# All attention first, then one feed-forward run over all batches, with the attention output through DRAM

## The chip, the cores and the metric

The kernel runs on one core of a Trainium2 chip. The core has five engines with an instruction queue each, which they work through in order: TensorE (PE, matrix multiplication; its weight loads are shown as PEld), VectorE (DVE), ScalarE (ACT), GpSimd (POOL) and SyncE (SP), which here only issues DMA transfers. The metric is the device time of one execution in microseconds (us); less is better.

## The reference

The computation has two parts. The first is attention in which a query sees only the keys of its own hash bucket; the second is a feed-forward layer with a short convolution as a gate. There are 4 batches, 8 heads, 768 positions, head size 64, a model width of 512 and an inner width of 1024.

```python
q_bucket = sum over 6 bits of ((q @ proj) > 0) * 2**bit     # k_bucket likewise
mask = q_bucket[:, :, :, None] == k_bucket[:, :, None, :]
scores = where(mask, q @ k.T / 8, -1e9)
attn = exp(scores - max(scores))
attn = attn / (sum(attn) + 1e-9)
x = (attn @ v) with the heads side by side                  # (4, 768, 512)
h = maximum(x @ w_in, 0)                                    # (4, 768, 1024)
conv = conv_w[0] * h[s-1] + conv_w[1] * h[s] + conv_w[2] * h[s+1]
out = (h * sigmoid(conv)) @ w_out
```

The weights `w_in`, `w_out` and `conv_w` come as 64-bit floats, which the kernel decodes on the chip from their integer halves.

## The kernel before

**Work units.** Two heads of a batch form a pair; there are 16 pairs. Each pair has 12 units: a unit is 128 queries of one head against all 768 keys. Units run in groups of four (two heads, two blocks of 128 queries), so a pair has three groups and the kernel 48 groups. The main loop has one iteration per unit, and in each iteration the engines work on different units: `products` (line 286, four matmuls `s`) and `maximum` (lines 299 to 303) of unit i, `normalise` (lines 313 and 314) of unit i-1, and `transposes` (line 329, six transposes `t`) and `to_sbuf` (line 336, ScalarE copies them out) of unit i-3. `exponential` (line 306) is on ScalarE. Once in a group, in the iteration after its last transposes, `values` multiplies the group's transposed probabilities with v: 24 matmul records `v` of line 355 in a row, the burst. All of this is issued in the order of the loop, and each engine takes its instructions in this order.

**PSUM.** The products `s`, the transposes `t` and the hash of the next pair take turns in three PSUM slots of two banks each (`ring(ps, 3, ..., "S", ...)`). So the transposes of an iteration take the slot that the maximum of the iteration before has read, or an older one: the transposes of the third iteration of a group wait for the maximum of its second.

**Two kinds of normalisation.** The first six pairs (`LATE = NP + DEFER`) do not normalise the probabilities. They collect the sums (`reciprocals`), spread the reciprocals by two transposes (line 350), and multiply the values by them (`factors`, `out`: lines 360 to 366). The other ten pairs normalise each unit on GpSimd (line 314, in place, 128 x 768) and copy the values out in a high and a low part (lines 369 and 372). Both forms leave the attention output in SBUF, as a high part `xh` and a low part `xl`.

**Preparation of the next pair.** During a pair, `prepare` works on the next: `split` rounds the queries and keys on GpSimd (line 204, `hi`), subtracts (line 209, `R`, in place: the remainder) and lets SP copy the parts into their operand tiles by DMA (lines 207 and 211); `hash` computes the bucket bits (lines 219 to 228). The pieces come at iterations 1, 3, 4, 5 and 7 of the 12. The keys and queries of the pair after next are loaded at iteration 7 into the only tile `R` (line 191), after the DMAs that still read it.

**Decoding.** `split_weights` is a generator that decodes 16 blocks of weights. A block takes four vector steps on VectorE (lines 95, 97, 102 and 104), a size and a rounding on ScalarE (lines 87 and 136), a clamp on GpSimd (line 90), and a subtraction and an addition on GpSimd (`ends`, lines 139 and 140), which are issued halfway through the next block. `background(RATE)` takes 3.75 steps in every burst iteration from iteration 7; the rest falls in the first feed-forward. `fetch` loads the raw blocks from ScalarE's queue.

**Feed-forward.** `ffn(b, ...)` runs after two pairs of the next batch have been done, so four times, between attention pairs. It has 16 steps, one for half of the positions and one of eight blocks of 128 inner columns. A step has `hidden` (line 393, 12 matmuls `h`, then ScalarE and VectorE for the gate, lines 398 to 411, then GpSimd, line 412) and, three steps later (`FLAG`), `output` (line 423, 9 matmuls `o` that add up in PSUM). At the start ScalarE loads the table of the sigmoid, at the end that of the exponential (line 435).

The loop's central lines:

```python
        if u:
            u.maximum(prev)
        ...
        if prev and prev.pair.late:
            prev.normalise()
        ...
        next(prep[0], None)
        for _ in range(1 + NCK if ending else AVS[(i - LAG) % 4]):
            ...                       # the burst: values
        if burst and i >= W0:
            background(RATE)
```

Of the kernel before, what the change touches and what calls it, by code (L numbers as in the profile page):

```python
# [17 lines left out]
P = 128  # L18
# [3 lines left out]
QB = 256  # L22
# [9 lines left out]
DEFER = 2  # L32
FLAG = 3
LATE = NP + DEFER
AVS = (1 + NCK, 0, 0, 0)
PREP = 1
PREP_N = 6
W0 = 7
RATE = 3.75
# [4 lines left out]
def lsh_attention_conv_ffn(ctx, tc, qk, v, hw, w_in, conv_w, w_out, consts, ident_in, out):  # L44
# [113 lines left out]
    fetched, due, taps = [], [0], []  # L158
# [10 lines left out]
    def background(n):  # L169

        due[0] += n
        while due[0] >= 1:
            due[0] -= 1
            next(weights_todo, None)


    class Pair:
        def __init__(self, b, p):
            self.b, self.p, self.nm = b, p, f"{b}_{p}"
            self.late = b * NP + p >= LATE  # L180
            self.rec = None
# [92 lines left out]
    class Unit:  # L274
# [14 lines left out]
        def maximum(self, prev):  # L289

            self.st = ring(wp, 8, [P, 4], F32, "st", f"st{self.nm}")
            pr = self.pair
            if self.tq == 0 and self.h == 0 and not pr.late:
                pr.sums = ring(wp, 3, [P, QB // P, 2], F32, "sums", f"sums{self.nm}")
            self.sums = None if pr.late else pr.sums
            self.sum = self.st[:, 2:3] if pr.late else pr.sums[:, self.tq, self.h:self.h + 1]
# [4 lines left out]
            if prev and prev.pair.late:  # L301
                prev.total()
            nc.vector.tensor_scalar(self.st[:, 1:2], self.st[:, 0:1], -SCALE, None, ALU.mult)  # L303

        def exponential(self):
            nc.scalar.activation(self.e, self.e, AF.Exp, bias=self.st[:, 1:2], scale=SCALE,  # L306
                                 accum_out=self.sum)

        def total(self):
            nc.vector.tensor_scalar(self.sum, self.sum, 1e-9, None, ALU.add)  # L310

        def normalise(self):
            nc.vector.reciprocal(self.st[:, 3:4], self.sum)
            nc.gpsimd.tensor_scalar(self.e, self.e, self.st[:, 3:4], 0.0, ALU.mult, ALU.add)  # L314

        def reciprocals(self):

            pr = self.pair
            sums = self.sums
            nc.vector.tensor_scalar(sums, sums, 1e-9, None, ALU.add)  # L320
            nc.vector.reciprocal(sums, sums)
            pr.rec = ring(wp, 1, [P, QB // P, 2, D], F32, "rec", f"rec{self.nm}")
            nc.gpsimd.tensor_scalar(pr.rec, sums.unsqueeze(3).to_broadcast([P, QB // P, 2, D]), 1.0, 0.0,
                                    ALU.mult, ALU.add)
# [14 lines left out]
    def values(pr, qb, ats, rec):  # L339

        if qb == 0:
            pr.x = [ring(wp, NP + DEFER, [P, S], F32R, f"x{k}", f"x{k}{pr.nm}")
                    for k in "hl"]
        vt, (xh, xl) = pr.v, pr.x
        av = ring(ps, 2, [P, 512], F32, "M", f"v{pr.nm}_{qb}")

        def spread():

            for t in range(QB // P):
                nc.tensor.transpose(av[:, QB + t * P:QB + (t + 1) * P],  # L350
                                    rec[:, t].rearrange("p h d -> p (h d)"), ident)

        def chunk(c):
            for h in range(2):
                nc.tensor.matmul(av[h * D:(h + 1) * D, :QB], vt[:, c, h, :],  # L355
                                 ats[h][:, c // 3, c % 3, :],
                                 start=(c == 0), stop=(c == NCK - 1), tile_position=(0, h * D))

        def factors():
            nc.scalar.copy(rs, av[:, QB:2 * QB])  # L360

        def out():
            x = ring(wp, 1, [P, QB], F32, "x32", f"x{pr.nm}_{qb}")
            nc.vector.tensor_tensor(x, av[:, :QB], rs, ALU.mult)
            nc.gpsimd.tensor_scalar(xh[:, cols], x, 1.0, 0.0, ALU.mult, ALU.add)
            nc.gpsimd.tensor_tensor(xl[:, cols], x, xh[:, cols].bitcast(F32), ALU.subtract)

        def out_high():
            nc.scalar.copy(xh[:, cols], av[:, :QB])

        def out_low():
            nc.vector.tensor_tensor(xl[:, cols], av[:, :QB], xh[:, cols].bitcast(F32), ALU.subtract)

        cols = slice(qb * QB, (qb + 1) * QB)
        chunks = [lambda c=c: chunk(c) for c in range(NCK)]
        if pr.late:
            return chunks, (out_high, out_low)
        rs = ring(wp, 1, [P, QB], F32, "rs", f"rs{pr.nm}_{qb}")
        return [spread, *chunks], (factors, out)


    g2, prep = [None], [iter(())]

    def hidden(b, half, f, xs):
# [4 lines left out]
        for c in range(NCC):  # L389
            xh, xl = xs[c]  # L390
# [23 lines left out]
    def output(b, half, f, g, acc):  # L414
        if f == 0:
            acc[half] = [ring(ps, 3, [P, 2, 512], F32, "S", f"o{b}_{half}_{k}")
                         for k in range(2)]
        for m in range(HS // P):
            op = acc[half][m // 2][:, m % 2, :]
            gh, gl = (g[:, k, m * P:(m + 1) * P] for k in range(2))  # L420
            wh, wl = (weights[f"o{f}"][:, k, :] for k in range(2))
            for n, (l, r) in enumerate(((gh, wh), (gh, wl), (gl, wh))):
                nc.tensor.matmul(op, l, r, start=(f == 0 and n == 0),  # L423
                                 stop=(f == NFC - 1 and n == 2))
        if f == NFC - 1:
            for m in range(HS // P):
                osb = ring(wp, 5, [P, WC], I32, "wl", f"osb{b}_{half}_{m}").bitcast(F32)
                copy = nc.vector.tensor_copy if m == 2 else nc.scalar.copy
                copy(osb, acc[half][m // 2][:, m % 2, :])
                r0 = half * HS + m * P  # L430
# [168 lines left out]
```

## Time and profile before

| | |
|---|---|
| median of 3 runs | 754.43 us (751.63 to 755.96) |
| span of the profiled execution | 749.0 us; its own device time is not listed apart from the three |
| TensorE | busy 714.4 us (95%), 4588 matmuls |
| VectorE, ScalarE, GpSimd | busy 499.2, 509.2 and 373.6 us |
| mean granted TensorE clock | 0.984 |
| DMA | 72.18 MB, mean 96 GB/s |

The span is from the first to the last instruction of the profile; the device time holds what lies around it as well. Lines of the profile name an engine, an operation, the tile written and the tile read, and numbers after `x` are counts. A `<-` in brackets after "idle before" names what ended an engine's wait. Matmuls are pipelined, so their single durations overlap; starts are the safer measure. "PE v L355 x24" is one burst.

### The profile page before, as it was taken

The page shows a single profiled execution, that of the slowest core. Times are in us where ns is not written, and L with a number is a line of the kernel's source. Part 1 is how long each engine was busy: PE and PEld are TensorE (multiplying, and loading weights), DVE is VectorE, ACT ScalarE, POOL GpSimd, SP SyncE. Part 2 cuts the span into 40 slices and gives each one's busy share as a digit, 9 for nine tenths or more (in the row PEclk, how much of TensorE's full clock was granted, in tenths as well). Part 3 has the DMA queues.
Part 4 walks back from the last instruction along what each step waited for, and adds up shares of the span by engine and source line. Part 5 has one row for each costly group of instructions (what it writes and reads, how often), then busy time and mean ns, then how long its engine had stood idle before and what let it go on. Part 6 is the DMA issues. An engine that isn't in the chain of part 4 may idle for free.

```text
span 749.0 us, 13385 instructions
## 1 busy us (share of the span) xinstructions
PE 714.4 (95%) x4588; PEld 587.5 (78%) x4588; DVE 499.2 (67%) x1195; ACT 509.2 (68%) x954; POOL 373.6 (50%) x372
## 2 busy tenths in 40 slices
PE   5989999988899999999999999999999999999997
PEld 3767777776679987777788988777788897778986
DVE  7588999977667656666657655665666665564663
ACT  5867887886655548778774557787785547785554
POOL 4366777756566324755735423656645323341221
PEclk8999999998999999999999999999999999999999
DMA  3876576553412102365441302255461211000011
GB/s 141 198 204 155 141 206 181 168 162 85 114 43 72 64 37 70 82 181 136 121 121 31 104 1 105 68 150 132 119 163 33 70 43 63 2 1 1 0 43 43
DMA packets 30357, 72.18 MB, mean 96 GB/s; under 512 B 5937, under 2 KB 7505, under 8 KB 30289
## 3 DMA queue, kind: packets, MB, share of 16 engines
q1 hardware_dynamic: 27696, 62.88, 30.9%
q10 hardware_dynamic: 2592, 8.44, 3.6%
q8 instruction: 37, 0.61, 0.3%
q14 instruction: 32, 0.25, 0.1%
HBM read 27.40 MB, written 6.29 MB: 45 GB/s over the span
## 4 chain that ended last, share of the span: by engine, by line
PE 69%; DVE 4%; POOL 4%; DMA 3%; ACT 1%; issue 1%; SPq 0%; POOLq 0%; DVEq 0%
PE o L423 18%; PE h L393 17%; PE s L286 11%; PE t L329 11%; PE v L355 11%; DVE e L299 2%; DMA k<-R 1%; DMA R<-in_qk 1%; PE hash L219 1%; POOL wuo L139 1%; POOL e L314 1%; POOL wo L140 1%; ACT e L306 1%; DVE wuo L97 1%; POOL R L209 1%
## 5 line engine op out<-in xcount | busy, mean ns | idle before, releaser
L299 DVE TENSOR_SCALAR_CACHE_REDUCE e<-s 128x768 f32<-128x768 f32 x192 | 183.3, 955 | 80.9 <-PE s L286 72.1
L306 ACT ACTIVATE e<-e,st 128x768 f32<-128x768 f32 x192 | 181.2, 944 | 23.1 <-DVE st L303 12.8
L336 ACT COPY at<-t 128x768 f32<-128x768 f32 x192 | 152.3, 794 | 47.3 <-PE t L329 47.1
L329 PE MATMUL t<-ident,e 128*128 128x128 f32 x1152 | 164.5, 280 | 19.9 <-DVE e L299 17.9
L314 POOL TENSOR_SCALAR e<-e,st 128x768 f32<-128x768 f32 x120 | 109.3, 911 | 117.3 <-ACT at L336 59.9
L329 PEld LDWEIGHTS t<-ident,e 128*128 128x128 f32 x1152 | 133.4, 144 | 42.6 <-DVE e L299 22.4
L402 DVE SCALAR_TENSOR_TENSOR ht<-ht,cw 128x384 f32<-128x384 f32 (+1 forms) x128 | 117.8, 921 | 70.0 <-ACT ht L400 66.8
L412 POOL TENSOR_TENSOR g<-ht,g 128x384 fp32r<-128x384 f32 x64 | 72.0, 1125 | 163.9 <-ACT g L411 129.7
L423 PE MATMUL o<-wo,g 128*128 128x512 f32 x576 | 143.3, 395 | 0.7 <-POOL g L412 0.7
L393 PE MATMUL h<-xh,wi 128*128 128x386 f32 x512 | 142.0, 340 | 0.0
L355 PE MATMUL v<-at,v 128*64 128x256 f32 x1152 | 134.9, 383 | 0.0
L423 PEld LDWEIGHTS o<-wo,g 128*128 128x128 f32 x576 | 107.0, 188 | 23.5 <-ACT ht L400 1.2
L286 PE MATMUL s<-K,Q 128*128 128x384 f32 x384 | 118.7, 391 | 1.0 <-POOL K L253 0.9
L355 PEld LDWEIGHTS v<-at,v 128*64 128x64 f32 x1152 | 78.7, 137 | 45.5 <-issue 10.9
L286 PE MATMUL s<-k,q 96*128 96x384 f32 x384 | 102.2, 348 | 2.2 <-DVE e L299 2.2
L405 ACT ACTIVATE ht<-ht 128x384 f32<-128x384 f32 x64 | 33.6, 525 | 96.4 <-DVE ht L402 96.4
L393 PEld LDWEIGHTS h<-xh,wi 128*128 128x128 f32 x512 | 94.0, 188 | 3.7 <-ACT ht L400 1.2
L393 PE MATMUL h<-xl,wi 128*128 128x386 f32 x256 | 86.8, 339 | 0.0
L286 PEld LDWEIGHTS s<-K,Q 128*128 128x128 f32 x384 | 60.1, 196 | 22.2 <-issue 17.4
L286 PEld LDWEIGHTS s<-k,q 96*128 96x128 f32 x384 | 72.9, 197 | 3.0 <-ACT q L266 3.0
L406 DVE TENSOR_TENSOR ht<-ht 128x384 f32<-128x384 f32 x64 | 41.5, 649 | 31.5 <-ACT ht L405 31.3
L209 POOL TENSOR_TENSOR R<-R,hi 128x768 fp32r<-128x768 f32 x30 | 60.4, 2014 | 0.9 <-PE hash L219 0.8
(75 smaller groups left out, 622.2 us busy)
## 6 DMA issues: line engine op xcount, KB each, us to landing
R<-in_qk SPq DMA_DIRECT2D x15, 768.0 KB
K<-hi SPq DMA_DIRECT2D x60, 192.0 KB
v<-in_v SPq DMA_DIRECT2D x16, 384.0 KB
out<-osb SPq DMA_DIRECT2D x24, 256.0 KB
Q<-hi SPq DMA_DIRECT2D x30, 192.0 KB
q<-hi SPq DMA_DIRECT2D x30, 192.0 KB
Q<-R SPq DMA_DIRECT2D x30, 192.0 KB
k<-R SPq DMA_DIRECT2D x30, 192.0 KB
```

The source lines that it names most:

```text
L209: nc.gpsimd.tensor_tensor(lo, R, hi.bitcast(F32), ALU.subtract)
L286: nc.tensor.matmul(self.sp[:, half, :HS], A[:, h, qs], C[:, h, half * HS:(half + 1) * HS], start=(kk == 0), stop=(kk == 1))
L299: nc.vector.tensor_scalar(self.e.rearrange("p (a b) -> p a b", a=2), self.sp[:, :, :HS], MASKED, None, ALU.max, ALU.max, accum_out=self.st ...
L306: nc.scalar.activation(self.e, self.e, AF.Exp, bias=self.st[:, 1:2], scale=SCALE, accum_out=self.sum)
L314: nc.gpsimd.tensor_scalar(self.e, self.e, self.st[:, 3:4], 0.0, ALU.mult, ALU.add)
L329: nc.tensor.transpose(self.tp[:, c // 3, c % 3 * P:(c % 3 + 1) * P], self.e[:, c * P:(c + 1) * P], ident)
L336: nc.scalar.copy(pr.at[self.h][:, :, :, self.tq * P:(self.tq + 1) * P], self.tp[:, :, :3 * P].rearrange("p j (c q) -> p j c q", c=3))
L355: nc.tensor.matmul(av[h * D:(h + 1) * D, :QB], vt[:, c, h, :], ats[h][:, c // 3, c % 3, :], start=(c == 0), stop=(c == NCK - 1), tile_posi ...
L393: nc.tensor.matmul(hp[:, :HW], w, x[:, c0:c0 + HW], start=(n == 0), stop=(n == 3 * NCC - 1))
L402: nc.vector.scalar_tensor_tensor(t[:, a:z], ht[:, o + k - 1 + a:o + k - 1 + z], cw[:, f, k:k + 1], t[:, a:z], ALU.mult, ALU.add)
L412: nc.gpsimd.tensor_tensor(g[:, 1, :], t, g[:, 0, :].bitcast(F32), ALU.subtract)
L423: nc.tensor.matmul(op, l, r, start=(f == 0 and n == 0), stop=(f == NFC - 1 and n == 2))
```

## The change

- All 16 pairs of attention run one after the other. All of them normalise each unit on GpSimd; the sums, the spreading and the factors of the first six pairs are gone.
- The output of a burst is copied once by VectorE (128 x 256), in the following iteration, and stored by SP to DRAM (`xd`).
- `feed_forward` is one run of 64 steps over all batches, started when the last products are issued, so that its first three steps stand among the last iterations of attention. It holds six output accumulators in the three PSUM slots, used half by half in turn.
- The attention output of a batch is loaded from DRAM by `load_x` and split into high and low parts by `split_x` on GpSimd: for the first batch during pairs 8 and 9, for the others during the feed-forward of the batch before.
- A step of the decoding is taken in every second iteration from iteration 14; a raw block is fetched in every sixth iteration.
- The tables are no longer switched back and forth between attention and feed-forward: the sigmoid's is loaded once.

```diff
-LATE = NP + DEFER
-AVS = (1 + NCK, 0, 0, 0)
-W0 = 7
-RATE = 3.75
+DECODE = 14
+FETCH = 6
+X0 = 8
...
     def exponential(self):
         nc.scalar.activation(self.e, self.e, AF.Exp, bias=self.st[:, 1:2], scale=SCALE,
-                             accum_out=self.sum)
+                             accum_out=self.st[:, 2:3])
...
-    def values(pr, qb, ats, rec):
+    def values(pr, qb, ats):
...
         def out():
-            x = ring(wp, 1, [P, QB], F32, "x32", f"x{pr.nm}_{qb}")
-            nc.vector.tensor_tensor(x, av[:, :QB], rs, ALU.mult)
-            nc.gpsimd.tensor_scalar(xh[:, cols], x, 1.0, 0.0, ALU.mult, ALU.add)
-            nc.gpsimd.tensor_tensor(xl[:, cols], x, xh[:, cols].bitcast(F32), ALU.subtract)
-
-        def out_high():
-            nc.scalar.copy(xh[:, cols], av[:, :QB])
-
-        def out_low():
-            nc.vector.tensor_tensor(xl[:, cols], av[:, :QB], xh[:, cols].bitcast(F32), ALU.subtract)
+            x = ring(wp, 2, [P, QB], F32, "x32", f"x{pr.nm}_{qb}")
+            nc.vector.tensor_copy(x, av[:, :QB])
+            nc.sync.dma_start(xd[pr.b][pr.p][:, qb * QB:(qb + 1) * QB], x)
...
+    def load_x(b):
+        xs = []
+        for c in range(NCC):
+            if b % 2 == 0:
+                x = ring(wp, NCC, [P, 2, S], F32R, "x", f"x{b}_{c}")
+            else:
+                x = ring(wp, 2, [P, 2, S], F32R, ("Q1", "K1")[c % 2], f"x{b}_{c}")
+            nc.sync.dma_start(x[:, 1].bitcast(F32), xd[b][c])
+            xs.append(x)
+        return xs
+
+    def split_x(xs):
+        for x in xs:
+            raw = x[:, 1].bitcast(F32)
+            nc.gpsimd.tensor_scalar(x[:, 0], raw, 1.0, 0.0, ALU.mult, ALU.add)
+            yield
+            nc.gpsimd.tensor_tensor(x[:, 1], raw, x[:, 0].bitcast(F32), ALU.subtract)
+            yield
...
+    def feed_forward(x0):
+        gs, run, xs, splits = [], [], x0, iter(())
+        load_table(AF.Sigmoid)
+        todo = [(b, half, f) for b in range(B) for half in range(2) for f in range(NFC)]
+        per = 2 * NFC
+        for i in range(len(todo) + FLAG):
+            if i % per == 0 and i < len(todo):
+                if i:
+                    xs = nxt
+                if i // per + 1 < B:
+                    nxt = load_x(i // per + 1)
+                    splits = split_x(nxt)
...
+            if i % per >= 4:
+                next(splits, None)
+            yield
...
-    for i in range(n + LAG):
+    for i in range(n + LAG + 1):
...
-        if burst and i >= W0:
-            background(RATE)
...
+        if i % FETCH == FETCH - 1:
+            fetch(1)
+        if i >= DECODE and i % 2 == 0:
+            next(weights_todo, None)
+        if pi == X0 and k == 0:
+            x0 = load_x(0)
+            splits = split_x(x0)
+        if x0 and k % 3 == 2:
+            next(splits, None)
+        if i == n:
+            tail = feed_forward(x0)
+        if tail:
+            next(tail)
```

More of the change, by code (lines that the diff above doesn't have):

```diff
@@ L300, in maximum @@
                                     MASKED, None, ALU.max, ALU.max, accum_out=self.st[:, 0:1])
-            if prev and prev.pair.late:
+            if prev:
                 prev.total()
@@ L384, in hidden @@
+            nc.vector.tensor_copy(x, av[:, :QB])
+            nc.sync.dma_start(xd[pr.b][pr.p][:, qb * QB:(qb + 1) * QB], x)
+        return out
+    g2, prep, acc = [None], [iter(())], []
+    xd = [[tc.dram_tile([P, S], F32, name=f"xd{b}_{c}") for c in range(NCC)] for b in range(B)]
     def hidden(b, half, f, xs):
@@ L421, in output @@
             wh, wl = (weights[f"o{f}"][:, k, :] for k in range(2))
[L422 to L430, printed above, removed]
-                nc.sync.dma_start(out[b, r0:r0 + P, :], osb)
+            for i, (l, r) in enumerate(((gh, wh), (gh, wl), (gl, wh))):
+                nc.tensor.matmul(op, l, r, start=(f == 0 and i == 0),
+                                 stop=(f == NFC - 1 and i == 2))
@@ L433, in load_table, with store @@
+    def store(b, n, half):
+        for m in range(HS // P):
+            k = n * 3 + m
+            osb = ring(wp, 5, [P, WC], I32, "wl", f"osb{b}_{half}_{m}").bitcast(F32)
+            copy = nc.vector.tensor_copy if m == 2 else nc.scalar.copy
+            copy(osb, acc[k // 2][:, k % 2, :])
+            r0 = half * HS + m * P
+            nc.sync.dma_start(out[b, r0:r0 + P, :], osb)
     def load_table(func):
         nc.scalar.activation(spare, cst[:, 0:1], func)
-    def ffn(b, xs, fill, last):
-        gs, acc, run = [], {}, []
+    def feed_forward(x0):
+        gs, run, xs, splits = [], [], x0, iter(())
@@ L507, in lsh_attention_conv_ffn @@
             u.exponential()
-        if prev and prev.pair.late:
+        if prev:
             prev.normalise()
@@ L518, in lsh_attention_conv_ffn @@
         next(prep[0], None)
-        for _ in range(1 + NCK if ending else AVS[(i - LAG) % 4]):
-            if av:
-                steps, last = av[0]
-                steps.pop(0)()
-                if not steps:
-                    outs.append(last)
-                    av.pop(0)
-        if burst and i >= W0:
-            background(RATE)
+        if av:
+            outs.append(values(*av))
+            av = None
+        if burst:
+            av = w.pair, w.qb, w.pair.at
         if u and k == PREP + PREP_N and pi + 1 < len(pairs):
@@ L535, in lsh_attention_conv_ffn @@
             next(g, None)
-        fetch(i % 2 if i < 8 else burst)
-        if w and w.tq == QB // P - 1 and w.h == 1:
-            if not ending:
-                av.append(values(w.pair, w.qb, w.pair.at, w.pair.rec))
-            else:
-                def fill():
-                    steps, last = values(w.pair, w.qb, w.pair.at, w.pair.rec)
-                    for step in [*steps, *last]:
-                        step()
-                bi = ffn_after[wi]
-                early = units[i + 1 - LAG] if i + 1 - LAG < n else None
-                def transposes_ahead():
-                    if early:
-                        early.transposes()
-                        early.to_sbuf()
-                        turns["S"] -= 1
-                ffn(bi, [pairs[bi * NP + c].x for c in range(NCC)], fill, transposes_ahead)
+        if i % FETCH == FETCH - 1:
[11 more added lines that the diff above has]
+            next(tail)
+    for o in outs:
+        o()
+    for _ in tail:
+        pass
 def kernel(q, k, v, proj, moe_w_in, moe_conv_w, moe_w_out):
```

113 lines of the change are left out of this document (26 added, 87 removed).

## The prediction

> **What bounds the kernel now.** I read the page first, then the windows of three stretches, the chain of work in order of time, and last the timeline of single instructions.
>
> ```profile
> PE 714.4 (95%) x4588; PEld 587.5 (78%) x4588; DVE 499.2 (67%) x1195; ACT 509.2 (68%) x954; POOL 373.6 (50%) x372
> ...
> PEclk8999999998999999999999999999999999999999
> ```
>
> TensorE is busy for 95% of the span, so only 35 us can be idle, and whatever the change gains must lie there or in slow stretches. The windows say where those are: the early attention with the decoding in it, one late group of four units, and a piece of feed-forward.
>
> ```profile
> 24.76:197.68 172.92, 154.00 (x1097) 122.05 (x1096) 140.65 (x307) 129.78 (x241) 115.14 (x118) 0.95 0.61 167
> 285.42:293.95 8.53, 8.53 (x67) 6.98 (x68) 5.17 (x21) 7.00 (x14) 3.70 (x5) 1.00 0.00 0
> 397.13:441.40 44.27, 44.27 (x221) 39.85 (x220) 30.14 (x37) 22.96 (x46) 18.55 (x16) 1.00 0.21 57
> ```
>
> The columns are length, then PE, PEld, DVE, ACT and POOL busy, the granted clock and DMA. Early, TensorE lacks 18.9 us of 172.9 and its clock is 0.95; late, it lacks nothing. The chain gives the lengths:
>
> ```profile
> 197.75 2.74 PE v L355 x24
> ...
> 285.42 2.76 PE v L355 x24
> 293.95 2.74 PE v L355 x24
> 303.24 2.74 PE v L355 x24
> ...
> 397.13 2.10 PE o L423 x9
> ...
> 676.49 2.74 PE v L355 x24
> ...
> 736.40 8.28 PE o L423 x36
> ```
> ```profile
> 24.76 2.81 PE L355 MATMUL v<-at,v 128*64 128x256 f32 x24
> ```
>
> A `v` burst comes once in four units, so its starts are a ruler. A late group takes 293.95 - 285.42 = 8.53 us, and 9.29 with the pair's hash in it (0.76 more). The 17 early groups from 24.76 to 197.75 take 173.0, or 10.17 each. With six hashes in them (4.6) they exceed the late rate by 23.4 us. That is the early loss. The first feed-forward costs little: from 197.75 to 285.42 are 87.7 us, two groups (17.1) and 70.6. Pure feed-forward is, from the third window with eleven `o` of 2.10 and ten `h`, h = (44.27 - 23.1)/10 = 2.12, so 16 steps of 4.22 = 67.5. The stage change costs some 3 us the first time and less later. So the change can win about 30 us: the early loss, and few us from stage changes.
>
> **The floor of the new kernel.** All 48 bursts come in attention, at iterations 7, 11, ... 195. To the first burst 24.8 as before; 46 groups at 8.53 = 392.4; 14 hashes at 0.76 = 10.6; the drain from iteration 191 to 195 has a burst, four sets of transposes (0.6 each, from 291.70 below to the next products) and three `h`: 2.74 + 2.4 + 6.4 = 11.5, less some overlap, 10.9; from the last burst on 2.74 + 61 x 2.12 + 64 x 2.10 = 266.5, and the tail behind the last `o`, 749.0 - (736.40 + 8.28) = 4.3; one wait of the first `o`, 0.8. (The same terms for 676.49 to the end of before, 2.74 + 15 x 2.12 + 16 x 2.10 + 4.3 = 72.4, meet the measured 72.5.) Sum 710.3. One early wait stays, since the third pair's keys are loaded as before:
>
> ```profile
> 46.96 0.85 PE L219 MATMUL hash<-R,hw_sb 128*32 128x384 f32 x8 [1.02 <-DMA R<-in_qk]
> ```
>
> By the ruler that hash could come near 24.8 + 2 x 8.53 = 41.8. Fewer weight fetches run beside the load now, so I take 4 of these 5 us. The floor is 714.3, against a span of 749.0.
>
> **What the change puts on top.** Decoding now takes one step in every even iteration from 14, four vector steps per block of weights, so 16 blocks last 16 x 8 iterations: to about 146, eleven pairs and not fifteen. Numbering the iterations of a group first to fourth, with the burst in the fourth, steps fall in the first and third. In before they stood in the fourth, where VectorE has room. One late group shows the room:
>
> ```profile
> 289.21 0.96 DVE L299 TENSOR_SCALAR_CACHE_REDUCE e<-s 128x768 f32<-128x768 f32 x1 [2.57 <-PE s L286]
> ...
> 290.28 0.16 DVE L313 RECIPROCAL st<-st 128x1 f32<-128x1 f32 x1
> ...
> 290.56 0.96 DVE L299 TENSOR_SCALAR_CACHE_REDUCE e<-s 128x768 f32<-128x768 f32 x1
> 290.63 0.91 POOL L314 TENSOR_SCALAR e<-e,st 128x768 f32<-128x768 f32 x1 [2.89 <-ACT at L336]
> ...
> 291.44 0.08 DVE L299 DVE_READ_ACCUMULATOR e<-s 128x1 f32 x1
> ...
> 291.70 0.82 PE L329 MATMUL t<-ident,e 128*128 128x128 f32 x6
> ...
> 297.71 0.96 DVE L299 TENSOR_SCALAR_CACHE_REDUCE e<-s 128x768 f32<-128x768 f32 x1 [2.28 <-PE s L286]
> ```
>
> The transposes at 291.70 reuse the PSUM slot that the maximum of 290.56 reads, which is done at 291.52. Between the reciprocal's end (290.44) and that maximum are 0.12 us, between the maximum's end and the transposes another 0.18. The slack of the first iteration is 0.3 us; that of the fourth is 2.28. Prices:
>
> ```profile
> L97 DVE SCALAR_TENSOR_TENSOR wui<-rawi,wli x8: 681/868/2120, 37.9 to 111.4; 128x512 int32<-128x512 int32 x8
> L104 DVE SCALAR_TENSOR_TENSOR wlo<-rawo,wlo x8: 681/820/2182, 130.1 to 216.7; 128x512 f32<-128x512 uint32 x8
> L102 DVE TENSOR_SCALAR wlo<-wuo x8: 417/916/1940, 122.8 to 212.7; 128x512 int32<-128x512 int32 x8
> L372 DVE TENSOR_TENSOR xl<-v,xh 128x256 fp32r<-128x256 f32 x30 | 12.2, 408 | 6.5 <-ACT xh L369 6.5
> L139 POOL TENSOR_TENSOR wuo<-wuo,wo 128x512 f32<-128x512 f32 x8 | 11.2, 1406 | 1.7 <-ACT wo L136 1.7
> L140 POOL TENSOR_TENSOR wo<-wuo,wlo 128x512 fp32r<-128x512 f32 x8 | 10.9, 1360 | 0.6
> L90 POOL TENSOR_SCALAR wlo<-wlo 128x512 f32<-128x512 f32 x8 | 6.4, 803 | 0.7
> L209 POOL TENSOR_TENSOR R<-R,hi 128x768 fp32r<-128x768 f32 x30 | 60.4, 2014 | 0.9 <-PE hash L219 0.8
> L204 POOL TENSOR_SCALAR hi<-R 128x768 fp32r<-128x768 f32 x30 | 26.1, 870 | 17.0 <-DMA R<-in_qk 9.7 <-DMA K<-hi 3.0 <-PE h L393 1.7
> ```
>
> *First-iteration steps.* These are L97 and L104, two per block. The new copy of the attention output stands there too; its nearest row is L372, 0.41, of which 0.30 delay the next instruction. At its shortest a step takes 0.68, 0.60 of it its own. So the second maximum starts (0.30 + 0.60 - 0.12) = 0.78 late, its transposes 0.6 late, of which the burst's own wait for ScalarE gives 0.1 back: 0.5 us in each of 32 groups, 16 us. Bounds: nothing if the steps hide; 32 x 1.0 = 32 us if they last as long as they did on average beside GpSimd's work. I take the short end, because the row at 290.63 shows GpSimd waiting just before, so VectorE usually gets in first. The steps of the third iteration fall before the burst, 2.28 us of room, at nothing. Where a group has no decoding the copy uses 0.3 of 0.3: 1.5 us over 15 groups.
>
> *GpSimd.* Every pair is now normalised on GpSimd (0.91 a unit), with 72 units more than before. The second half of a block's decoding (L139, L140, the clamp) is issued in the third iteration, 16 times: 1.41 + 1.36 + 0.80 = 3.6 us in front of that group's last normalisations. Behind it stands, at iteration 7 of a pair (5 times) and 3 (6 times), the key remainder of 1.8 to 2.0 (L209), and then the normalisation that the next group's third transposes need. From the normalisation of the third iteration on, GpSimd has 0.9 + 3.6 + 0.9 + 1.9 + 0.9 + gaps 0.5 = 8.7 us to do. In the quoted group the normalisation of the first iteration starts at 290.63, those of the second and third each some 1.5 later, as the maxima do, so this chain starts 3.2 + 0.4 (the shift above) behind 290.63, at 294.2, and ends at 302.9. The transposes of the next group's third iteration would start at 291.70 + 8.53 + 0.5 = 300.7, or 301.5 where a hash stands between. The stalls are 2.2 and 1.4, of which 0.5 is counted already: 1.7 x 5 + 0.9 x 6 + 0.1 x 5 for the blocks that meet no remainder = 14.4, say 14 us. Bounds: nothing, if the longer groups let GpSimd catch up; 25 if VectorE's step also waits for the remainder to end, as it did once:
>
> ```profile
> 122.16 2.31 POOL L209 TENSOR_TENSOR R<-R,hi 128x768 fp32r<-128x768 f32 x1
> ...
> 122.82 1.94 DVE L102 TENSOR_SCALAR wlo<-wuo 128x512 int32<-128x512 int32 x1
> ```
> ```profile
> 125.69 0.88 PE L329 MATMUL t<-ident,e 128*128 128x128 f32 x6 [0.95 <-DVE e L299]
> ```
>
> There a step of 0.42 became 1.94 beside L209, and TensorE stood 0.95.
>
> *The clock.* A stall also slows the matmuls behind it:
>
> ```profile
> 31.59 0.87 PE L329 MATMUL t<-ident,e 128*128 128x128 f32 x6 [1.75 <-DVE e L299]
> ...
> 33.83 1.48 PE L329 MATMUL t<-ident,e 128*128 128x128 f32 x6
> ```
> ```profile
> 86.78 0.88 PE L329 MATMUL t<-ident,e 128*128 128x128 f32 x6 [1.54 <-DVE e L299]
> ...
> 88.20 0.82 PE L329 MATMUL t<-ident,e 128*128 128x128 f32 x6
> ```
>
> After 1.75 us of idling six transposes take 1.48 instead of 0.82; after 1.54 they don't. An episode doubles about 1.6 us of work. The five stalls at iteration 7 (2.2) lie not far above that edge, and my estimate of them is no better than that; I count half of them, 4 us. The Trainium skill ("TensorE: Matmul & The Clock Gate", Part 1) lets the clock fall only after an idle window of about 3.4 us; by that these 4 us would be nothing and the sum 4 lower. The trace's 1.75 us contradicts it here, at least as a limit for a single gap.
>
> *The attention output through DRAM.* Removed: two instructions per burst on ScalarE/GpSimd, and 36 transposes. Added: 48 stores and 16 loads on SP. Loading and splitting the first batch falls in pairs 8 and 9: four times 0.87 + 2.01 = 11.5 us of GpSimd beside its pile-ups, and 1.5 MB of loads beside the keys. Half shows: 6 us (bounds 0 and 11.5). The other three batches split under feed-forward, where GpSimd is busy 18.55 of 44.27 and another 0.7 per step fits; if that cover went, it would be 3 x 11.5. A store waits in SP's order for VectorE's copy, with the key DMAs behind it, and the chain already showed that loop full once:
>
> ```profile
> 346.03 5.25 DMA k<-R
> 351.33 4.08 DMA R<-in_qk
> ```
>
> One more issue per group there: 2 us over the last pairs (0 to 5). One fetch is used one iteration after its issue (the third block, iterations 17 and 18): 1 us. Weight decoding gone from the first feed-forward is already in the floor.
>
> **Sum.** 714.3 + 16 + 1.5 + 14 + 4 + 6 + 2 + 1 = 758.8, against 749.0: 9.8 more. What lies around the span isn't shown for the profiled execution; the runs' median 754.43 is 5.4 above it. So 764.2, about 764, 1.3% slower.
>
> **The rivals.**
> 1. *Decode steps hide (faster).* If VectorE's steps of the first iteration fit, the terms 16 and 1.5 go, and the pile-ups that they push against the transposes (14 + 4) halve: 758.8 - 26.5 = 732, so 737 us. It decides at 0.3 us: a step that starts so early, or a transpose that waits so little, costs nothing. For it: VectorE is busy only 5.17 of 8.53 in a late group; against: the rows at 290.28 to 291.70.
> 2. *Every pile-up goes over the clock's edge (much slower).* VectorE's steps wait for the remainders as at 122.82 (the upper bound of 25 instead of 14), all eleven stalls then pass 1.7 us and add 11 x 1.6 = 18 instead of 4: 758.8 + 25 = 784, so 789 us at the outside; half of it, 776, is where it begins. For it: the 0.95 clock in the early window. Against: iteration 3 has the hash's 0.76 as room.
> 3. *Gain and cost cancel (same).* Steps at their shortest and GpSimd catching up half of its pile-ups: 758.8 - 9 = 750, so 755 us.
>
> **How the numbers follow.** Forecast (758.5 to 775) 0.42, hiding 0.23, clock 0.20, cancelling (750.7 to 758.2) 0.15. Faster by over 0.5% (about what a measurement of this kernel can tell from no change) 0.23, within 0.15, slower 0.62. The range reaches to rival 1's own time, 737, and to 786 in rival 2, and leaves about half of each, 2 in 10, out.
>
> **What would show it.** Right: groups of 9.0 to 9.2 us between bursts while decoding lasts (to iteration 146) and 8.5 to 8.7 after; `t` waiting for the maximum once a group, by half a microsecond; groups of 10.5 and more where iteration 7 follows a block's end; `t` waiting for `e` of GpSimd; a feed-forward of 64 steps at 4.22 without gaps. Wrong: groups of 8.6 with decoding in them (rival 1), transposes of 1.48 all over pairs 2 to 12 (rival 2), or gaps in the feed-forward at batch changes, for which I counted nothing.

## The result, and the profile after

The changed kernel takes 763.61 us (median of 4 runs, 761.04 to 765.92); the kernel before took 753.85 us beside it (4 runs, 751.63 to 755.96). The ratio is 1.0142, with a 95% interval of 1.0100 to 1.0184: slower, by about 10 us. The profiled execution is one of the longer ones, 765.89 us, with a span of 764.1 us and a mean clock of 0.985.

The page of the changed kernel, engine totals and the clock by slices:

```profile
PE 711.3 (93%) x4552; PEld 579.4 (76%) x4552; DVE 489.6 (64%) x1303; ACT 486.2 (64%) x892; POOL 448.4 (59%) x422
...
PEclk8999999999999989999999999999999999999999
```

TensorE has 3 us less work than before in a span 15 us longer (the medians differ by 10 us), so its idle time grew from 35 to 53 us in these two executions. The clock is hardly the place: its one dip in the middle is a single slice, around 270 us. GpSimd has 75 us more to do. The waits of TensorE, first for the attention part (24 to 470 us) and then from there to the end, say where the idle time ends:

```profile
PE t L304 <- DVE st L295: 26.5, 32, 1.8
PE t L304 <- POOL e L299: 5.5, 5, 2.9
PE hash L209 <- DMA R<-in_qk: 1.9, 4, 1.0
```
```profile
PE h L342 <- DVE x L324: 2.7, 1, 2.7
PE v L319 <- ACT at L311: 2.1, 1, 2.1
```

The columns are the sum in us, the count and the longest one. The transposes `t` waited 32 times for VectorE (L295 is a small step right behind the maximum that frees their slot). 32 is also the number of decoding steps that fall in first iterations. The chain of the changed kernel gives the ruler again, burst to burst:

```profile
193.00 2.74 PE v L319 x24
202.15 2.74 PE v L319 x24
...
326.68 2.74 PE v L319 x24
337.26 2.74 PE v L319 x24
...
439.22 2.74 PE v L319 x24
447.94 2.74 PE v L319 x24
...
474.09 2.74 PE v L319 x24
```

A late group without decoding takes 447.94 - 439.22 = 8.72 us, where the kernel before took 8.53. A group with step L96 in its first iteration takes 9.15. The group behind iteration 7 of a pair, where a block's end stands right ahead of the remainder on GpSimd, takes 10.58. Three timelines of the changed kernel show what stands behind each. The late group:

```profile
417.07 0.41 DVE L324 COPY x<-v 128x256 f32<-128x256 f32 x1
...
417.40 0.15 DVE L298 RECIPROCAL st<-st 128x1 f32<-128x1 f32 x1
```

The copy of the attention output pushes the reciprocal, and behind it the next maximum, by 0.33 us. The group with L96:

```profile
119.07 0.68 DVE L96 SCALAR_TENSOR_TENSOR wui<-rawi,wli 128x512 int32<-128x512 int32 x1
...
119.35 1.16 POOL L299 TENSOR_SCALAR e<-e,st 128x768 f32<-128x768 f32 x1 [1.32 <-DVE st L298]
...
119.66 0.95 DVE L284 TENSOR_SCALAR_CACHE_REDUCE e<-s 128x768 f32<-128x768 f32 x1
...
120.76 0.41 PE L304 MATMUL t<-ident,e 128*128 128x128 f32 x2 [0.51 <-DVE st L295]
```

The decoding step of 0.68 us stands between copy and maximum, and TensorE idles 0.51 us for the maximum. GpSimd, which had waited, starts its normalisation within that step and takes 1.16 us for it instead of 0.91. The group behind a block's end:

```profile
145.25 1.27 POOL L139 TENSOR_TENSOR wi<-wui,wli 128x512 fp32r<-128x512 f32 x1
...
148.06 1.83 POOL L199 TENSOR_TENSOR R<-R,hi 128x768 fp32r<-128x768 f32 x1
...
148.34 2.11 DVE L103 SCALAR_TENSOR_TENSOR wli<-rawi,wli 128x512 f32<-128x512 uint32 x1
...
149.88 1.34 POOL L299 TENSOR_SCALAR e<-e,st 128x768 f32<-128x768 f32 x1
...
150.37 0.94 DVE L284 TENSOR_SCALAR_CACHE_REDUCE e<-s 128x768 f32<-128x768 f32 x1
...
151.47 0.85 PE L304 MATMUL t<-ident,e 128*128 128x128 f32 x6 [1.75 <-DVE st L295]
```

GpSimd ends the block (L139), and its remainder L199 then starts 0.28 us ahead of VectorE's L103. That step takes 2.11 us instead of 0.67 and ends 0.56 us after L199 has ended. The maximum behind it is late, and TensorE idles 1.75 us. By duration the two kinds of step behave differently, as the lines of the changed kernel grouped by source show (minimum, median, maximum in ns):

```profile
L96 DVE SCALAR_TENSOR_TENSOR wui<-rawi,wli x8: 673/674/676, 59.5 to 198.2; 128x512 int32<-128x512 int32 x8
L103 DVE SCALAR_TENSOR_TENSOR wli<-rawi,wli x8: 672/1782/2150, 68.7 to 207.4; 128x512 f32<-128x512 uint32 x8
```

L96 always takes 0.67; in the row at 119.07 it starts ahead of GpSimd, which had been waiting. L103, of the same shape, takes up to 2.15: in the row at 148.34 GpSimd had work ready behind a block's end and started first. In groups with a hash no remainder stands ahead of L103, and in four of these five it takes 0.67 to 0.68. The Trainium skill ("SBUF — State Buffer", section "SBUF: two separate sides", on the port pair that VectorE and GpSimd share) says that a VectorE operation with two SBUF inputs and a GpSimd operation that reads SBUF exclude each other, and that the first to start holds the ports to its end. The 2.11 us behind a remainder that began first agree with it. The normalisation at 119.35 agrees in kind: it is 0.25 us longer, where L96 still had 0.40 us to run.

At the change of stage, the windows of the changed kernel (length; PE, PEld, DVE, ACT, POOL busy; clock; DMA) and two single instructions:

```profile
485.25:500.00 14.75, 10.02 (x48) 6.68 (x47) 7.11 (x10) 5.18 (x10) 3.18 (x3) 0.86 0.00 1
560.00:620.00 60.00, 60.00 (x302) 54.34 (x301) 40.23 (x45) 30.79 (x60) 29.03 (x23) 1.00 0.13 45
```
```profile
487.98 4.42 PE L319 MATMUL v<-at,v 128*64 128x256 f32 x22 [2.08 <-ACT at L311]
...
499.51 3.80 PE L342 MATMUL h<-x,wi 128*128 128x386 f32 x12 [2.66 <-DVE x L324]
```

TensorE lacks 4.7 us around the last burst and runs at a clock of 0.86; the 22 matmuls of the burst take 4.42 where 24 take 2.74. In the long feed-forward it lacks nothing, at 4.22 us a step.

### The profile page after: what moved, and what is told of

It is laid out like the page before. It is cut to its first block, busy times and chain, and to the rows that moved or that the text cites. A ratio compares the mean times of both kernels' runs of the same rounds, so it can differ in the third digit from the quotient of the medians.

```text
span 764.1 us, 13725 instructions
## 1 busy us (share of the span) xinstructions
PE 711.3 (93%) x4552; PEld 579.4 (76%) x4552; DVE 489.6 (64%) x1303; ACT 486.2 (64%) x892; POOL 448.4 (59%) x422
## 4 chain that ended last, share of the span: by engine, by line
PE 66%; DVE 19%; DMA 5%; POOL 4%; issue 3%; ACT 2%; SPq 1%; DVEq 0%; POOLq 0%; ACTq 0%
PE o L391 17%; PE h L342 17%; PE v L319 15%; DVE e L284 10%; PE s L276 8%; PE t L304 7%; DMA R<-in_qk 3%; POOL e L299 2%; DMA k<-R 2%; DVE wli L103 1%; DVE wlo L103 1%; PE hash L209 1%; DVE st L298 1%; DVE st L288 1%; DVE st L295 1%
## 5 line engine op out<-in xcount | busy, mean ns | idle before, releaser
L299 POOL TENSOR_SCALAR e<-e,st 128x768 f32<-128x768 f32 x192 | 186.1, 971 | 114.8 <-DVE st L298 98.5
L304 PE MATMUL t<-ident,e 128*128 128x128 f32 x1152 | 162.9, 278 | 33.4 <-DVE st L295 26.5
L304 PEld LDWEIGHTS t<-ident,e 128*128 128x128 f32 x1152 | 131.0, 142 | 62.1 <-POOL e L299 52.1
L342 PE MATMUL h<-x,wi 128*128 128x386 f32 x768 | 147.7, 341 | 2.7 <-DVE x L324 2.7
L342 PEld LDWEIGHTS h<-x,wi 128*128 128x128 f32 x768 | 138.0, 190 | 8.9 <-DVE x L324 3.1
L319 PE MATMUL v<-at,v 128*64 128x256 f32 x1152 | 137.8, 387 | 2.1 <-ACT at L311 2.1
L276 PE MATMUL s<-K,Q 128*128 128x384 f32 x384 | 116.3, 384 | 1.5 <-POOL K L243 1.2
L276 PE MATMUL s<-k,q 96*128 96x384 f32 x384 | 99.8, 341 | 2.3 <-DVE e L284 2.1
L276 PEld LDWEIGHTS s<-K,Q 128*128 128x128 f32 x384 | 58.6, 192 | 21.8 <-issue 18.9
L355 DVE TENSOR_TENSOR ht<-ht 128x384 f32<-128x384 f32 x64 | 47.5, 741 | 33.7 <-ACT ht L354 33.7
L347 ACT ACTIVATE ht<-h 128x386 f32<-128x386 f32 x64 | 31.6, 494 | 37.3 <-PE h L342 37.1
L199 POOL TENSOR_TENSOR R<-R,hi 128x768 fp32r<-128x768 f32 x30 | 54.8, 1828 | 0.0
```

Of the source, the lines that this page charges most:

```text
L199: nc.gpsimd.tensor_tensor(lo, R, hi.bitcast(F32), ALU.subtract)
L276: nc.tensor.matmul(self.sp[:, half, :HS], A[:, h, qs], C[:, h, half * HS:(half + 1) * HS], start=(kk == 0), stop=(kk == 1))
L304: nc.tensor.transpose(self.tp[:, c // 3, c % 3 * P:(c % 3 + 1) * P], self.e[:, c * P:(c + 1) * P], ident)
L319: nc.tensor.matmul(av[h * D:(h + 1) * D, :QB], pr.v[:, c, h, :], ats[h][:, c // 3, c % 3, :], start=(c == 0), stop=(c == NCK - 1), tile_po ...
L342: nc.tensor.matmul(hp[:, :HW], w, x[:, c0:c0 + HW], start=(n == 0), stop=(n == 3 * NCC - 1))
```

## The experiments

Eleven kernels ran in three sets, each set on one chip with runs of the kernel before (medians 750.35, 750.41 and 751.6 us). Ratios are to the kernel before on the same chip; the changed kernel stands at 1.0142 in the first comparison and at 1.0182 in the control. Spans are of one profiled execution each and scatter by up to 5 us between executions of one kernel, so single groups are read from the chain.

**Set 1: the four disputed places, one edit each.**

*Decoding steps in the third and fourth iteration of a group.*

```diff
-        if i >= DECODE and i % 2 == 0:
+        if i >= DECODE and i % 4 >= 2:
```

> The changed kernel, with the vector steps of the decoding in the third and fourth iteration of each group instead of the first and third; as many steps per group as now. Theory A (place of the steps, and GpSimd's queue by itself): the groups that hold L96 fall from 9.15 to the 8.72 of the groups without decoding (16 x 0.43 = 7 us), the groups behind a block's end lose the part in which L103 waits beside the remainder L199, but keep some 1 us each because GpSimd still has the block's end and the remainder ahead of a normalisation; together 13 to 18 us less, a time of 746 to 750. Rival B (only VectorE's delayed steps count, GpSimd's queue is hidden): all groups at 8.7 to 8.9, the 33 us above 8.72 all gone, 728 to 733. Rival C (the decoding costs its engine time wherever it stands): no change, 760 to 766.

Measured: 761.25 us, ratio 1.0152 (1.0115 to 1.0189). Waits of TensorE in this kernel:

```profile
PE t L304 <- POOL e L299: 17.5, 21, 2.4
PE hash L209 <- DMA R<-in_qk: 11.4, 9, 3.2
```

The wait for VectorE fell from 26.5 us to two waits of 0.4, and of the groups without a hash that had L96 in them all but two fell to 8.71 to 8.79. That much of the first theory holds. But the groups behind iteration 7 and a block's end stayed at 10.4, because GpSimd's own queue now ended last, and hashes of the next pair waited for their keys, up to 3.2 us. The time gained is at most some 2.5 us, not the 13 to 18 that the first theory expected. The time lies in the range of rival C, but not for its reason: the wait was real, and two others stood right behind it. The longest of the hash waits, in this kernel's timeline, has four loads of the feed-forward's input (`x<-xd`) issued right behind the keys' load; the other eight hash waits, 0.4 to 1.9 us, are shorter:

```profile
245.74 0.39 SPq L181 DMA_DIRECT2D R<-in_qk  x1
...
247.17 2.43 SPq L371 DMA_DIRECT2D x<-xd  x4
...
252.65 1.35 PE L209 MATMUL hash<-R,hw_sb 128*32 128x384 f32 x8 [3.18 <-DMA R<-in_qk]
```

*The copy of the attention output on ScalarE.*

```diff
-            nc.vector.tensor_copy(x, av[:, :QB])
+            nc.scalar.copy(x, av[:, :QB])
```

> The changed kernel, with the copy of the attention output (128 x 256) on ScalarE instead of VectorE. Theory A (the copy stands between reciprocal and maximum in the first iteration, 0.41 us on VectorE): groups without decoding fall from 8.72 to 8.53, those with L96 from 9.15 to about 8.9; 46 groups by 0.2 = 9 us less, 754 to 756. Rival B (the 0.19 comes from GpSimd's or SP's larger load): groups stay at 8.72 and the time at 761 to 766. Rival C (ScalarE, now with 0.37 more per group, delays the copy of the transposes): slower than 766.

Measured: 756.21 us, ratio 1.0062 (1.0033 to 1.0091). Its chain:

```profile
443.44 2.74 PE v L319 x24
451.95 2.74 PE v L319 x24
```

A late group is 8.51 us again, the one with L96 8.82 instead of 9.15. So the copy costs 0.2 us in a group without decoding and 0.33 beside L96. 46 x 0.19 = 8.7 us is worked out from the first; the medians differ by 7.4 us, and by the ratios it is 6 to 9.

*The feed-forward started two iterations later.*

```diff
-        if i == n:
+        if i == n + 2:
```

> The changed kernel, with the feed-forward started two iterations later, so that one of its steps and not three stands before the last burst. Theory A (in the drain ScalarE's in-order queue holds the last copies of transposes behind the table load and the first gates, so that the last burst waits 2.1 us, the fourth step 2.7 us, and the clock halves for some 4 us): the stretch from the last burst to the end shrinks from 278.9 by about what the late steps cost, less two steps (8.4 us) that now come behind the burst; from the burst of iteration 191 to the end (290.1 now) 282 to 286, so 4 to 8 us less, 756 to 760. Rival B (the wait is the latency of the drain, which then lies bare): the same to within 2 us.

Measured: 764.51 us, ratio 1.0178 (1.0145 to 1.0212). From the burst before the last to the end are 288.4 us, against 290.1; the first `h` waits 4.8 us for the last copy, against 2.7. The time is that of rival B: the stage change costs the same, with its idle time in another place.

*The first batch's feed-forward input loaded and split in the last pairs.*

```diff
-X0 = 8
+X0 = 13
```

> The changed kernel, with loading and splitting of the first batch's attention output in pairs 13 and 14 instead of 8 and 9, where no decoding is left. Theory A (it is the meeting of the splitting with a block's end and the remainder on GpSimd that makes the group of 14.95 us in pair 8): that group falls to 10.6, the next ones by some 0.3 each, and the groups of pairs 13 and 14 rise by 0 to 0.5: 4 to 7 us less, 756.5 to 759.5. Rival B (the loads or the splitting cost their 11.5 us of GpSimd wherever they stand): the same to within 2 us, with a long group in pair 13 or 14.

Measured: 760.47 us, ratio 1.0138 (1.0108 to 1.0167), a span of 759.1. In the changed kernel one group of pair 8 (pairs are counted from 0) had taken 14.95 us; its timeline shows why:

```profile
262.17 1.82 POOL L381 TENSOR_TENSOR x<-x 128x768 fp32r<-128x768 f32 x1
...
269.43 0.87 PE L304 MATMUL t<-ident,e 128*128 128x128 f32 x6 [2.93 <-POOL e L299]
...
272.10 1.54 PE L304 MATMUL t<-ident,e 128*128 128x128 f32 x6 [0.81 <-POOL e L299]
```

A piece of the split (L381, 1.82 us) runs on GpSimd ahead of the block's end, and the normalisations behind that end come late: TensorE idles 2.93 us, and the next transposes take 1.54. With the split moved, the same group in the chain of this kernel takes 10.57:

```profile
262.74 2.74 PE v L319 x24
273.31 2.74 PE v L319 x24
```

The 4.4 us of that group are gone, and two groups of pairs 13 and 14 that got the split are 0.3 and 0.7 us longer. The first theory's cause holds; the gain, some 3 us, is less than its 4 to 7.

**Set 2: control, the size of the decoding, and the waits that the first set uncovered.**

*The changed kernel once more.*

> The changed kernel once more, unaltered, so that the others of this set stand beside it on the same chip. All theories: 1.010 to 1.018 times the kernel before.

Measured: 763.78 us, ratio 1.0182 (1.0159 to 1.0205), a span of 761.4. The pattern of groups is the same; the one of pair 8 is 12.65 instead of 14.95, so its length varies between executions. In a group of pair 9 (L103 beside a remainder) the transposes behind an idle time go at half rate, which they did not at the same place in the first profile:

```profile
291.90 1.51 PE L304 MATMUL t<-ident,e 128*128 128x128 f32 x6 [1.74 <-DVE st L295]
```

*Two weight blocks decoded instead of sixteen.*

```diff
-            fetched.append((raw, name))
+            if name in ("i0_0", "i1_0"):
+                fetched.append((raw, name))
...
-            wh, wl = (weights[f"i{c}_{fb}"][:, k, fo:fo + P] for k in range(2))
+            wh, wl = (weights[f"i{c % 2}_0"][:, k, fo:fo + P] for k in range(2))
...
-            wh, wl = (weights[f"o{f}"][:, k, :] for k in range(2))
+            wh, wl = (weights[f"i{f % 2}_0"][:, k, :] for k in range(2))
```

> The changed kernel, with 2 of the 16 blocks of weights decoded and these two used in place of all, so that the matmuls of the feed-forward are the same in number and shape; all blocks are still loaded. Theory A (the decoding's vector steps in the first iteration and its GpSimd work make the groups of 9.15 to 10.6): from pair 3 on groups fall to 8.72, with a hash to 9.5; 14 of 16 blocks' share of 7 + 26 us is 29 us less, a span of 733 to 738, a ratio of 0.975 to 0.985. Rival B (the keys' load loop R-remainder-DMA-load sets the pace of a pair as soon as the groups get shorter): hashes wait for R once per pair by 1 to 2 us, groups with a hash at 10 to 11, only 10 to 18 us less. The long group of pair 8 should fall to about 11 in both, since no block's end is there.

Measured: 741.11 us, ratio 0.9883 (0.9849 to 0.9918), 22.7 us below the control. From pair 3 on, the groups without a hash are 8.70 to 8.83, but for two in pairs 8 and 9 that have the split beside them, 9.59 and 9.05. Waits:

```profile
PE t L305 <- DVE st L296: 3.4, 6, 1.3
PE hash L210 <- DMA R<-in_qk: 3.1, 4, 1.1
```

So fourteen blocks cost 22.7 us, between the two expectations. Without them this kernel takes 1.2% less than the kernel before. That one still decodes all sixteen, so this does not compare the two orders without decoding; it shows that what the change wins elsewhere is less than what the decoding costs in the new order.

*Steps in the third and fourth iteration, and a second buffer for the keys.*

```diff
-            self.R = ring(wp, 1, [P, 2, S], F32R, "R", f"R{nm}")
+            self.R = ring(wp, 2, [P, 2, S], F32R, "R", f"R{nm}")
...
-        if i >= DECODE and i % 2 == 0:
+        if i >= DECODE and i % 4 >= 2:
```

> The kernel with the vector steps in the third and fourth iteration, and a second buffer for the keys and queries R, so that the load of the pair after next no longer waits for the DMAs out of the remainder. In the run without it the hash waited 11.4 us for R in 9 pairs. Theory A (that loop took back what the moved steps had won): these waits go, groups with a hash at 9.5 to 10.4, 8 to 11 us less than without the buffer, a ratio near 1.00 to 1.005. Rival B (R lands late because the DMA engines and SP's issues are full, not because of the buffer): waits stay above 7 us and the ratio at 1.011 to 1.018. The waits of transposes for GpSimd's e (17.5 us) stay in both.

Measured: 752.08 us, ratio 1.0018 (0.9996 to 1.0040), 9.2 us less than with the steps moved alone. Waits:

```profile
PE t L304 <- POOL e L299: 15.4, 19, 2.6
PE hash L209 <- DMA R<-in_qk: 1.5, 3, 0.9
```

The wait for keys fell from 11.4 to 1.5 us, and the time and the ratio are those of the first theory. With one buffer, a load of keys can't begin before the DMAs that read the old ones are done; shorter groups had left them less time.

*The copy of the last burst issued ahead of that iteration's feed-forward step.*

```diff
+        if i == n + LAG:
+            for o in outs:
+                o()
+            outs = []
         if tail:
             next(tail)
```

> The changed kernel, with one edit at the end of attention: the copy of the last burst is issued before the fourth step of the feed-forward and not behind it. Theory A (the fourth and fifth hidden matmuls wait 2.7 us because they take the PSUM slot of the last burst, whose copy stands behind that step's gate in VectorE's queue): that wait goes and the halved clock behind it shortens, 3 to 6 us less. Rival B (the gates' latency is next: the first outputs then wait for g instead): less than 1.5 us. The wait of the last burst for ScalarE's copy (2.1 us) stays in both.

Measured: 760.84 us, ratio 1.0135 (1.0111 to 1.0160), 2.9 us less than the control, just under the 3 to 6 of the first theory. The wait of `h` for the copy is gone; that of the last burst stays:

```profile
PE v L319 <- ACT at L311: 2.0, 1, 2.0
```

The copy had stood on VectorE behind the gate of the fourth step, in the in-order queue. Moving the copy that the last burst waits for, on ScalarE, was not tried.

**Set 3: the end of a block, and the edits together.**

*The block's subtraction where it was, its addition four iterations later.*

```diff
-                ends()
+                ends[0]()
...
             yield from d.lower()
+            if ends:
+                ends[1]()
```

> The changed kernel, with the two GpSimd instructions of a block's end issued apart: the subtraction where both stood, the addition four iterations later. VectorE's steps stay in the first and third iteration. Theory A (a normalisation waits behind block end and remainder on GpSimd, and L103 beside a remainder that comes late): 1.3 us less stand ahead of the remainder, so the groups behind iteration 6 fall from 10.6 to 9.2 to 9.6, those behind iteration 2 from 9.9 to 9.3, those with a hash from 11.0 to 10.2: 12 to 16 us less, a ratio of 0.997 to 1.003. Rival B (the moved addition delays the same transposes four iterations later): groups with L96 rise from 9.15 to 9.6 and more, the ratio stays above 1.010.

Measured: 755.12 us, ratio 1.0052 (1.0031 to 1.0072). Its chain at iteration 7 behind a block's end, its waits, and L103 by source:

```profile
316.57 2.74 PE v L322 x24
325.85 2.74 PE v L322 x24
```
```profile
PE t L307 <- DVE st L298: 18.9, 34, 1.7
```
```profile
L103 DVE SCALAR_TENSOR_TENSOR wli<-rawi,wli x8: 673/674/795, 68.8 to 203.2; 128x512 f32<-128x512 uint32 x8
```

Those groups fell from 10.6 to 9.3 us, and the wait for VectorE from the control's 25.8 to 18.9. L103 takes at most 0.80 us here (0.89 for the other weights), where it had taken up to 2.15 (2.25): with GpSimd's work parted, the long VectorE steps are gone too. The steps and the copy, which this edit leaves alone, keep the rest. The gain is 7 to 10 us, under the 12 to 16 of the first theory; rival B, a ratio above 1.010, is ruled out.

*Five edits together: steps in the third and fourth iteration, two buffers for the keys, the copy on ScalarE, the split in the last pairs, the last copy first.*

> Five edits together: vector steps in the third and fourth iteration, two buffers for R, the copy of the attention output on ScalarE, loading and splitting of the first batch in pairs 13 and 14, and the last copy ahead of the feed-forward's fourth step. If the gains of the single runs add (from 1.0018 for the first two: copy 9, splitting 5, last copy 3 us), 733 to 738 us, a ratio of 0.975 to 0.985, groups of 8.5 without a block's end and some 10.2 behind iteration 6. If the copy on ScalarE meets the size and the rounding of the decoding, or R's second buffer had already taken up what the late splitting wins, 742 to 747, 0.99 to 0.995.

Measured: 741.6 us, ratio 0.9869 (0.9836 to 0.9901). That lies between the two expectations, so the gains of the single runs do not add up in full. Late groups are 8.51, but many groups with a block's end ahead of them are 10.1 to 13.2. The waits of this kernel, and two sets of transposes in its timeline at half rate, the first right behind such a wait:

```profile
PE t L304 <- POOL e L299: 15.7, 24, 1.1
```
```profile
319.28 1.42 PE L304 MATMUL t<-ident,e 128*128 128x128 f32 x6 [1.10 <-POOL e L299]
...
321.78 1.35 PE L304 MATMUL t<-ident,e 128*128 128x128 f32 x6
```

*The same with the block's end split as well.*

> The five edits and the parted block end. What is left of decoding in the five are the transposes that wait for GpSimd, some 15 us. Theory A (the parted end takes most of them): 6 to 11 us below the five edits, 724 to 731 us, groups at 8.5 to 9.2, and with the 714 us of span worked out as floor, 5.4 to 15 above it. Rival B (the addition waits in the way elsewhere): within 3 us of the five edits.

Measured: 732.7 us, ratio 0.9749 (0.9717 to 0.9781): 2.5% faster than before, and some 4% faster than the change as it was made. Page and waits of this kernel:

```profile
PE 700.4 (96%) x4552; PEld 575.2 (79%) x4552; DVE 487.5 (67%) x1255; ACT 500.1 (68%) x940; POOL 448.8 (61%) x422
```
```profile
PE hash L212 <- DMA R<-in_qk: 7.0, 7, 1.8
PE t L307 <- POOL e L302: 5.2, 12, 1.0
```

This is 8.9 us below the five edits, as the first theory had it. Among the groups without a hash, those behind iteration 7 and a block's end are 9.02 to 9.07, the others behind a block's end 8.5 to 9.2, and nearly all that are left 8.45 to 8.6. Groups with a hash are 9.3 to 11.9, in part since hashes wait for their keys. GpSimd is busy as long as in the changed kernel (448.8 against 448.4); only the order of its work is different.

## Why the prediction was right, and where its sizes were off

The forecast was 764 us and slower; it is 763.6 and slower. That the decoding's steps and GpSimd's pile-ups would turn the sign was right, but the total is closer than its terms, and the stated range, 737 to 786 us, was wide. Taken from the profiled execution, in us:

| term | predicted | measured | how it is measured |
|---|---|---|---|
| to the first burst | 24.8 | 25.7 | chain |
| 46 groups at 8.53, 14 hashes | 403.0 | 403.2 | 46 x 8.53, 14 x 0.77 |
| copy in every group | 1.5 | 8.7 | 46 x (8.72 - 8.53), late groups taken for all |
| first-iteration decoding steps | 16 | 13.8 | 32 x 0.43, from 9.15 - 8.72, groups with L96 taken for all |
| GpSimd pile-ups | 14 | 14.7 | groups behind a block's end, over 8.72 + 0.43 and a hash; that of pair 8 taken as 10.55 |
| clock, and split beside pile-ups | 10 | 4.4 | the group of pair 8 over 10.55 |
| early wait, SP, a late fetch | 7 | 3.6 | what is left of the stretch |
| drain | 10.9 | 11.2 | chain |
| last burst to the end | 271.6 | 278.9 | chain |
| around the span | 5.4 | 1.8 | 765.89 - 764.1 |
| sum | 764.2 | 765.9 | |

**The floor** held: the group rate, the hash and the feed-forward's rate are as read from before. Where its work went off is the **stage change**. I counted "one wait of the first `o` 0.8" and it cost about 8: two waits of 2.1 and 2.7 us, and matmuls at half rate behind them. The late-group rows of before could not show it. What the step missed is that the gates of the first three feed-forward steps stand in ScalarE's and VectorE's queues ahead of the last copies of the attention; moving one of those copies gave 2.9 us back.

**First-iteration steps.** The slack of 0.3 us in that iteration, and that steps there push the next transposes, was right: 32 waits of `t` for VectorE, and all but 0.8 us of them gone when the steps left that iteration. The wait per step is 0.43, not 0.5. What was mis-sized is the **copy**: "0.3 of 0.3: 1.5 us over 15 groups". It stands in all 46 groups, since the steps come on top of it, and takes 0.2 in those without decoding; with the copy on ScalarE the group was at 8.51 again. Beside L96 it takes 0.33, so how the loss of such a group is shared between copy and step depends on which is taken away first.

**GpSimd.** The pile-ups cost 14.7 where 14 was worked out, and lie about where they were written: 7.1 behind iteration 7, 5.1 behind iteration 3, 2.5 in the groups with a hash. But most of it comes in the form that I had kept for the upper bound, VectorE's L103 waiting for the remainder. Transposes waited for GpSimd's `e`, the path that was worked out, only five times, 5.5 us in all and most of it in pair 8; for VectorE they waited 26.5 - 32 x 0.5 = 10.5 us beyond a plain step. The reason given, that VectorE usually gets in first, held for L96; of the 16 L103, ten took 1.4 to 2.25 us. Either path is late by about as much: taking VectorE's away left the groups at 10.4, and splitting the block's end brought them to 9.3. That the size came out right although the other path ended last is luck.

**Clock and split.** The 4 us of the clock did not show as predicted; in the profiled execution the transposes behind the stalls at iteration 7 went at 0.82 to 0.87, outside pair 8. The 6 us for the split were 4.4, in a single group, with half rate in it, and in the control about 2. The early terms and those of SP were too high.

**Around the span.** 5.4 us were taken from the runs' median less one span, which belong to different executions. 1.8 is what one execution has. Without that slip the forecast would have been 760.6. The 14.5 us missed in the stage change and the copy are made up, 11 by terms set too high (clock and split, early wait and SP, first-iteration steps) and nearly 4 by this one. That these misses cancel is luck.

Of the rivals, the one in which the steps hide is ruled out by the waits, the one of the clock by the full-rate transposes behind the stalls and the granted 0.985, and the one of cancelling by the ratio's interval, which starts at 1.0100. The loss of early groups is in the end no smaller than before: 23.4 us over the late rate in 17 groups then, 13.8 + 14.7 = 28.5 in more groups now. That the fourteen blocks not decoded gave 22.7 us back is near this sum (28.5 x 14/16 = 24.9), though some 3 of them lie in the group of pair 8.

In the other five kernels that decode every block, with its end in one piece, and keep the split in pair 8, that group was 14.1 to 14.6; in the three with the split moved it was 9.1 to 10.6. So the split's place is what makes it long. In the control, at 12.65, L103 took 0.67 us there instead of 1.53, and the transposes at half rate 1.54 and 1.09 instead of 1.54 and 1.48. What decides between the two forms stays open.

## What to carry to other kernels

Spreading background work over more iterations does not cheapen it; what counts is in which position of the pipeline it stands, and a position with 0.3 us of slack charged 0.43 of a step's 0.67 us each time. A sum of waits on one engine is not what their removal saves when other waits stand right behind: here 26 us of waits gave at most 2.5 until the second and third waits, a single key buffer and one long burst of GpSimd work, were taken away too. Price each place where work of two stages shares an in-order queue, the last copies of the old stage behind the first gates of the new one above all.

## What the runs showed of the hardware beyond that

The granted clock doesn't follow the length of a single gap. In the changed kernel six idle times of TensorE of 1.73 to 1.77 us left the matmuls behind them at full rate (the transposes at 151.47 take 0.85), while in the control, the same kernel, one of 1.74 us was followed by half rate (1.51 at 291.90). Before the change one of 1.75 us was, and in the kernel with five edits one of 1.10 us (1.42 at 319.28, 1.35 in the next set), though four others of 1.10 to 1.12 us there were not. What earlier load or idle time decides it, these runs don't settle.

Executions of one unaltered kernel differ by 0.6% in time: in the first comparison 765.9 us at a mean clock of 0.983 to 0.985 and 761.2 us at 0.995. In the control the time does not follow the mean clock (764.4 us at 0.994, 763.1 at 0.987). A difference under that is only to be read from medians, or from single groups.
